# Joining the words of the float64 weights: two VectorE operations and one more ScalarE operation in place of three VectorE operations

## The chip, the cores and the metric

One core of a Trainium2 chip runs the whole program. The metric is the device time in microseconds (us), the median of several runs. TensorE (PE) does matrix products, VectorE (DVE) and ScalarE (ACT) elementwise work, GpSimd (POOL) some more of it, and SyncE (SP) issues the DMAs. Each engine works through its own instructions in a fixed order, and waits at its first instruction that is not ready.

## The reference

Three layers follow each other. All inputs and the output are float32, except that the MLP's three weights are drawn as float64.

```python
# 1. random-feature attention, 4 batches, 8 heads, 576 tokens, width 64
proj = x @ w_phi; proj -= max(abs(proj))
phi(x) = concat(exp(proj), exp(-proj))
kv = phi(k).T @ v; z = sum(phi(k)); attn = (phi(q) @ kv) / (phi(q) @ z + 1e-6)
# 2. gated MLP on 2304 tokens, 512 -> 1536 -> 512
xn = x / rms(x) * rms_g
x = (silu(xn @ w_gate) * (xn @ w_val)) @ w_out
# 3. soft mixture of experts: 8 experts, 4 slots each
logits = x @ phi; slots = softmax(logits, tokens).T @ x
out = softmax(logits, slots) @ (relu(slots @ w1[e]) @ w2[e])
```

## The kernel before

**First stage, keys.** The 2304 tokens are 18 tiles of 128. For each tile and each half of its heads, PE projects the keys (`P`, line 392), DVE takes the largest absolute value (`mx`, line 396) and subtracts it (`pr`, line 400), ACT computes both exponentials (`kp`, lines 413 and 414), and PE adds to `kv` and `z` (`kacc`, lines 437 and 446). Between these stand the steps of the first block of 384 queries: PE `P` (line 320), DVE `qmx` and `qpr` (lines 323 and 324), PE transposes, ACT exponentials (line 337), then per pair of heads the numerator `num` and the denominator `den`, a reciprocal on DVE (line 217), eight copies on ACT (line 222) and a product on DVE (`xraw`, line 223).

**Second stage, MLP.** Six blocks of 384 tokens go through 12 column tiles each: `pg` and `pv` (line 795), `t` (tanh on ACT, line 802, two products on DVE, lines 803 and 807), a split of `t` into a high part `hh` (ACT, line 101) and a remainder `hl` (POOL or DVE, line 104), and the sum over columns `acc` (lines 820 to 822). The queries of the next block are worked on between them. The mixture of experts follows.

**The weights.** They arrive as float64 words and are needed as float32 pairs. There are 18 pieces of 128x1024, here called g0, v0, o0, g1, ... o5 (gate, value and out weight of pair 0 to 5). Pieces g0 to o2 are converted in the first stage, g3 to o5 in the first MLP block. For each piece:

- a DMA loads `wraw`, 128x1024 pairs of 32-bit words (line 122); `raw[:, :, 1]` is the high word, `raw[:, :, 0]` the low word;
- ACT reads the high word as float32 and scales it by 2^-112 into `wt` (`scale`, line 126), which turns an 11-bit exponent into an 8-bit one;
- DVE shifts `wt` left by 3 (line 133), ors the sign in (line 135), and ors the low word's three top bits in (line 137), one operation per call of `join`;
- `parts` splits `wt` into a rounded part (ACT, line 101) and a remainder (POOL, line 104), after which `wt`'s buffer is free.

In the first stage there are three buffers for `wraw` and two for `wt`; in the MLP there are two for `wraw`, and one for `wt` in each of two pools that take turns. The calls of `conv_load`, `conv_scale`, `conv_join` and `conv_parts` are strewn over the loops by hand, and a scheduler then sets the order of instructions on each engine.

Of the kernel before, what the change touches and what calls it, by code (L numbers as in the profile page):

```python
# [10 lines left out]
AF = mybir.ActivationFunctionType  # L11
ALU = mybir.AluOpType
# [12 lines left out]
MF = DFF // 128  # L25
NJ = MF // 2
NPRE = 9
KCONV, MCONV = (3, 2), (2, 1)
NX = 3
NLEFT = 2  # L30
# [9 lines left out]
def batch_parts(i):  # L40

    t0, parts = i * 128, []
    r = 0
    while r < 128:
        b = (t0 + r) // SEQ
        end = min(128, (b + 1) * SEQ - t0)
        parts.append((b, r, end))
        r = end
    return parts
# [14 lines left out]
def tile_kernel(ctx: ExitStack, tc: tile.TileContext, q2T, qT, kT, v, wbd, wg, wv, wo, rmsg, phi, w1, w2, consts, out):  # L64
    nc = tc.nc
    PE, DVE, ACT, POOL, SP = nc.tensor, nc.vector, nc.scalar, nc.gpsimd, nc.sync

    def pool(stack, name, space=None, bufs=1, side="left"):
        kw = {} if space is None else {"space": space}
        if space is None:  # L70
            kw["side"] = side
        if space is not DRAM:
            kw["reuse_waits"] = "tile"
        return stack.enter_context(tc.tile_pool(name=name, bufs=bufs, **kw))
# [37 lines left out]
    class Conv:  # L112
# [11 lines left out]
        def scale(self):  # L124
            self.w = self.wp.tile([128, 1024], F32, tag="S", name="wt", bufs=self.bufs[1])
            ACT.activation(out=self.w, in_=self.raw[:, :, 1].bitcast(F32), func=AF.Copy, scale=2.0 ** -112)

        def join(self):

            n = self.n = self.n + 1  # L130
            w, hi, lo = self.w.bitcast(U32), self.raw[:, :, 1], self.raw[:, :, 0]
            if n == 1:
                DVE.tensor_scalar(out=w, in0=w, scalar1=3, scalar2=None, op0=ALU.logical_shift_left)
            elif n == 2:
                DVE.scalar_tensor_tensor(out=w, in0=hi, scalar=0x80000000, in1=w, op0=ALU.bitwise_and, op1=ALU.bitwise_or)  # L135
            else:
                DVE.scalar_tensor_tensor(out=w, in0=lo, scalar=29, in1=w, op0=ALU.logical_shift_right, op1=ALU.bitwise_or)  # L137

        def parts(self):
            j, nm = self.key  # L140
# [4 lines left out]
    loaded, convs, joined = [], [], []  # L145

    def conv_load(sp, bufs, *pools):

        key = next(conv_at, None)
        if key is not None:  # L150
            c = Conv(sp, pools[pieces.index(key) % len(pools)], key, bufs)
            c.load()
            loaded.append(c)

    def conv_scale():
        if loaded:
            convs.append(loaded.pop(0))
            convs[-1].scale()

    def conv_join():  # L160
        if convs:
            convs[-1].join()
            if convs[-1].n == 3:
                joined.append(convs.pop())

    def conv_parts():
        if joined:
            joined.pop(0).parts()
# [199 lines left out]
    with ExitStack() as pk:  # L368
# [148 lines left out]
        for i in range(TILES):  # L517
            k, kn = ks[i], ks[i + 1] if i + 1 < TILES else None
            if i + 3 < TILES:
                ks[i + 3].load()  # L520
            if i + 2 < TILES:
                ks[i + 2].load_v()
            if i % 2 and i // 2 + 2 < NPRE:
                conv_load(sp, KCONV, sp)
            parts = batch_parts(i)
            b = parts[0][0]
            ends = i * 128 + parts[0][2] == (b + 1) * SEQ

            def finish():
                ev = Evac(b)  # L530
                fillers.extend([lambda n=n: ev.turn(n) for n in range(3)])

            if len(parts) > 1:
                k.kv(parts[0])
                finish()
            if kn:
                kn.project()
                kn.largest(0)
                if i % 2 == 0:
                    conv_join()  # L540
                kn.less(0)
                kn.largest(1)
                conv_join()
                kn.less(1)
            k.kv(parts[-1])
            for hf in range(2):
                if kn:
                    kn.exps(hf)
                if hf == 0 and i % 2:
                    conv_parts()  # L550
                    conv_scale()
                if fillers:
                    fillers.pop(0)()
                for f in qsteps[2 * i + hf]:
                    f()
            if ends and len(parts) == 1:
                finish()
# [23 lines left out]
    class Own:  # L581
# [6 lines left out]
        def fill(self, f, h, k0, k1):  # L588
            w = NS * self.k
            n = NE - 1  # L590
            h = h.rearrange("p k (e s) -> p e k s", e=NE)
            own = self.t[:, 0:n * (w + SPE)].rearrange("p (e x) -> p e x", e=n)[:, :, 0:w].rearrange("p e (k s) -> p e k s", s=NS)
            f(own[:, :, k0:k1, 0:SPE], h[:, 0:n])
            own = self.t[:, n * w:].rearrange("p (k s) -> p k s", s=NS)
            f(own[:, k0:k1, NS - SPE:], h[:, n])
# [8 lines left out]
    with ExitStack() as p2:  # L604
# [194 lines left out]
        def gate(m, xs):  # L799
            g = wide("g", m, xs)  # L800
            t = mp.tile([128, BLK], F32, tag="t", name="t", bufs=2)
            ACT.activation(out=t, in_=g, func=AF.Tanh, scale=0.5)  # L802
            DVE.scalar_tensor_tensor(out=t, in0=t, scalar=1.0, in1=g, op0=ALU.add, op1=ALU.mult)  # L803
            return t
# [30 lines left out]
        for blk in range(NBLK):  # L835
            acc = [ps.tile([128, DM], F32, tag=f"acc{i}", name=f"acc{i}", bufs=1) for i in range(TPB)]
            qsteps, qnext = qnext or [], None
            if blk == 1:
                tctx.close()
                q1ctx.close()  # L840
                qp = pool(qctx, "qp", side="right")
                q = Reduced(qp, ps, 2, {"misc": 3})
                q.begin()
                qsteps = q.steps()
                sp = pool(pctx, "post", side="right")
                S_run = stp.tile([128, 2 * DM], F32, tag="S", name="S_run", bufs=1)[0:96, 0:DM]
            if blk == NBLK - 1:
                pctx.close()
                qctx.close()
                kl = pool(ctx, "kl", side="right")  # L850
                xw = pool(ctx, "xw", bufs=NX, side="right")
                upool[:0] = [xw] * NX
                sp = pool(pctx, "post", side="right")
            if blk:
                x2 = []
                for i in range(TPB):
                    y = sp.tile([128, DM], F32, tag="x2", name="x2", bufs=TPB)
                    ACT.activation(out=y, in_=acc_done[i], func=AF.Copy, scale=0.5)
                    x2.append(y)
                steps = post(blk - 1, x2)  # L860
            plan = [[] for _ in range(3 * MF + 1)]
            for n, f in qsteps:
                plan[n].append(f)
            for n, f in zip(PSLOTS, steps):
                plan[n].append(f)
            done = [0]

            def fill():
                done[0] += 1
                if blk == 0:  # L870
                    n = (done[0] - 1) % CEVERY
                    if n == 0:
                        conv_parts()
                        conv_scale()
                    conv_join()
                    if n == 2:
                        conv_load(sp, MCONV, sp, stp)
                for f in plan[done[0] - 1]:
                    f()

            for m in range(MF):
                if m + 1 == MF and blk + 1 < NBLK:
                    xs = split_block(xraw.pop(blk + 1))
                more = m + 1 < MF or blk + 1 < NBLK
                if more:
                    t = gate((m + 1) % MF, xs)
                fill()
                if more:
                    val((m + 1) % MF, xs, t)
                fill()  # L890
                if more:
                    for i in range(TPB):
                        out_tile(m, hs, acc, i)
                if more:
                    hs = split_h(t, blk == 0 and m < MF - 3)
                fill()
                if blk == NBLK - 1 and m % 2 == 1:
                    unit(min(len(units) + (NX + 2 if m == 1 else 2), 17 + NX))
                if m == MF - 3 and 3 <= blk + 2 < NBLK:
                    q = Reduced(qp, ps, blk + 2, {"misc": 3})  # L900
                    q.begin()
                    qnext = q.steps()
            acc_done = acc
# [157 lines left out]
```

## Time and profile before

| | |
|---|---|
| median of 3 runs | 755.49 us (755.3 to 758.66) |
| the profiled execution | 756.4 us, of which the span of its instructions is 754.5 us |
| PE busy | 720.1 us, 95% of the span |
| DVE, ACT, POOL busy | 444.4 us (59%), 353.4 us (47%), 121.2 us (16%) |
| TensorE's granted clock, mean | 0.987 |

An engine's busy share is an average over stages. Which engine sets the end is read from each stage: how long PE, which is the busiest, stands idle there, and what ended each of these waits.

### The profile page before, as it was taken

The numbers are of one execution on the slowest core, as the hardware profiler recorded it, in microseconds if no ns is written. First come the engines' busy times: TensorE is split into PE (matmuls) and PEld (weight loads), VectorE is DVE, ScalarE is ACT, GpSimd is POOL, SyncE is SP. The second block draws the span as 40 slices with busy tenths as digits, with TensorE's granted clock in tenths as the row PEclk, the third lists the DMA queues.
The fourth block names the chain that finished last, engine by engine and source line by source line (L and its number), as shares of the span: only waits on it lengthen the run. The fifth ranks groups of instructions, "written<-read, shape, count | busy, mean of one in ns | idle before, by whom it ended". The sixth has DMA issues, their size and how long they took to land.

```text
span 754.5 us, 12364 instructions
## 1 busy us (share of the span) xinstructions
PE 720.1 (95%) x4919; PEld 577.8 (77%) x4919; DVE 444.4 (59%) x816; ACT 353.4 (47%) x787; POOL 121.2 (16%) x70
## 2 busy tenths in 40 slices
PE   7998998997999999999999999999999999999994
PEld 4554555876788888898888988889888899988343
DVE  5897967699846556455565555645556453333313
ACT  5658765455644556434564346643465331212102
POOL 0222210245510211012110121101211010000000
PEclk9998999999999999999999999999999999999997
DMA  8664211544101100101000010000100046567798
GB/s 311 233 233 168 84 44 45 188 152 156 56 15 62 38 23 22 47 1 32 22 22 20 1 32 22 23 18 1 32 1 2 9 168 242 204 235 282 280 374 315
DMA packets 25145, 79.45 MB, mean 105 GB/s; under 512 B 2688, under 2 KB 13376, under 8 KB 18688
## 3 DMA queue, kind: packets, MB, share of 16 engines
q1 hardware_dynamic: 24864, 77.79, 29.5%
q10 hardware_dynamic: 224, 0.88, 0.4%
q8 instruction: 38, 0.62, 0.3%
q14 instruction: 19, 0.16, 0.1%
HBM read 71.99 MB, written 6.67 MB: 104 GB/s over the span
## 4 chain that ended last, share of the span: by engine, by line
PE 75%; DVE 11%; DMA 5%; ACT 5%; issue 2%; POOL 0%; SPq 0%; ACTq 0%; DVEq 0%
PE pv L795 18%; PE pg L795 17%; PE acc L820 6%; PE acc L821 6%; PE acc L822 6%; PE num L204 4%; PE kacc L437 3%; DMA eu<-in_w_dram 2%; DVE wt L135 2%; PE P L392 2%; PE den L212 2%; DVE wt L137 2%; PE kacc L446 2%; DMA wraw<-in_wg_dram 2%; ACT e L222 1%
## 5 line engine op out<-in xcount | busy, mean ns | idle before, releaser
L795 PE MATMUL pv<-xnh,wv 128*128 128x384 f32 x576 | 151.5, 344 | 1.1 <-DVE t L807 1.1
L795 PE MATMUL pg<-xnh,wg 128*128 128x384 f32 x576 | 150.1, 342 | 0.2 <-ACT xnh L101 0.2
L795 PEld LDWEIGHTS pv<-xnh,wv 128*128 128x128 f32 x576 | 103.1, 188 | 8.6 <-issue 6.7
L795 PEld LDWEIGHTS pg<-xnh,wg 128*128 128x128 f32 x576 | 104.7, 188 | 5.9 <-ACT xnh L101 0.6
L795 PE MATMUL pv<-xnl,wv 128*128 128x384 f32 x288 | 97.7, 339 | 0.0
L795 PE MATMUL pg<-xnl,wg 128*128 128x384 f32 x288 | 97.5, 338 | 0.0
L278 POOL PARTITION_ALL_REDUCE qe<-qe x32 | 50.0, 1562 | 247.3 <-ACT qe L277 227.7
L820 PE MATMUL acc<-wo,hh 128*128 128x512 f32 x216 | 88.4, 409 | 1.0 <-ACT hh L101 0.9
L822 PE MATMUL acc<-wo,hl 128*128 128x512 f32 x216 | 85.5, 396 | 1.9 <-POOL hl L104 1.9
L821 PE MATMUL acc<-wo,hh 128*128 128x512 f32 x216 | 85.8, 397 | 0.0
L101 ACT CAST hh<-t 128x384 fp32r<-128x384 f32 x72 | 36.7, 510 | 85.6 <-PE acc L821 68.7
L803 DVE SCALAR_TENSOR_TENSOR t<-t,pg 128x384 f32<-128x384 f32 x72 | 39.7, 551 | 52.6 <-ACT t L802 52.5
L802 ACT ACTIVATE t<-pg 128x384 f32<-128x384 f32 x72 | 35.1, 487 | 63.2 <-PE pg L795 63.2
L104 DVE TENSOR_TENSOR hl<-t,hh 128x384 fp32r<-128x384 f32 x62 | 34.5, 557 | 48.0 <-ACT hh L101 45.5
L222 ACT COPY qe<-qe 32x192 f32<-32x192 f32 x128 | 44.8, 350 | 31.7 <-DVE qe L217 30.4
L807 DVE TENSOR_TENSOR t<-t,pv 128x384 f32<-128x384 f32 x72 | 39.7, 552 | 30.2 <-PE pv L795 28.9
L795 PEld LDWEIGHTS pg<-xnl,wg 128*128 128x128 f32 x288 | 54.0, 188 | 0.3 <-DVE xnl L104 0.3
L795 PEld LDWEIGHTS pv<-xnl,wv 128*128 128x128 f32 x288 | 54.0, 188 | 0.1
L822 PEld LDWEIGHTS acc<-wo,hl 128*128 128x128 f32 x216 | 40.6, 188 | 12.5 <-POOL hl L104 2.7
L437 PE MATMUL kacc<-kp,vt 128*64 128x256 f32 (+1 forms) x320 | 44.1, 400 | 4.0 <-ACT kp L414 4.0
L820 PEld LDWEIGHTS acc<-wo,hh 128*128 128x128 f32 x216 | 40.7, 189 | 9.2 <-ACT hh L101 2.0
L821 PEld LDWEIGHTS acc<-wo,hh 128*128 128x128 f32 x216 | 40.7, 188 | 6.4
(188 smaller groups left out, 1091.0 us busy)
## 6 DMA issues: line engine op xcount, KB each, us to landing
eu<-in_w_dram SPq DMA_DIRECT2D x32, 1024.0 KB, 6.2
wraw<-in_wg_dram SPq DMA_DIRECT2D x6, 1024.0 KB, 6.0
wraw<-in_wv_dram SPq DMA_DIRECT2D x6, 1024.0 KB, 6.3
wraw<-in_wo_dram SPq DMA_DIRECT2D x6, 1024.0 KB, 4.9
qraw<-in_qT_dram SPq DMA_DIRECT2D x32, 192.0 KB, 2.3
raw<-in_kT_dram SPq DMA_DIRECT2D x18, 256.0 KB, 4.0
vt<-in_v_dram SPq DMA_DIRECT2D x18, 256.0 KB, 3.2
out_dram<-ob SPq DMA_DIRECT2D x18, 256.0 KB, 3.4
```

Of the source, the lines that this page charges most:

```text
L101: ACT.copy(out=hi, in_=src)
L104: (lo_eng or POOL).tensor_tensor(out=lo, in0=src, in1=hi.bitcast(F32), op=ALU.subtract)
L222: ACT.copy(out=rd[64 * hh + 32 * r:64 * hh + 32 * r + 32, g], in_=dn[o:o + 32])
L278: POOL.partition_all_reduce(e[:, 0], e[:, 1], channels=128, reduce_op=bass_isa.ReduceOp.absmax)
L437: PE.matmul(out=kva[o0:o0 + 64, hh // 2], lhsT=self.vt[r0:r1, h], rhs=kp[r0:r1, hh].rearrange("p s f -> p (s f)"), start=first and hh < 2, ...
L795: PE.matmul(out=p, lhsT=w[:, a, c], rhs=x, start=n == 0, stop=n == 11)
L802: ACT.activation(out=t, in_=g, func=AF.Tanh, scale=0.5)
L803: DVE.scalar_tensor_tensor(out=t, in0=t, scalar=1.0, in1=g, op0=ALU.add, op1=ALU.mult)
L807: DVE.tensor_tensor(out=t, in0=t, in1=wide("v", m, xs), op=ALU.mult)
L820: PE.matmul(out=acc[i], lhsT=hh[:, s], rhs=w[:, 0], start=m == 0, stop=False)
L821: PE.matmul(out=acc[i], lhsT=hh[:, s], rhs=w[:, 1], start=False, stop=False)
L822: PE.matmul(out=acc[i], lhsT=hl[:, s], rhs=w[:, 0], start=False, stop=m == MF - 1)
```

## The change

The low word is no longer shifted by DVE. A second ACT operation, right after `scale`, reads it as an unsigned integer, multiplies it by 0.93 times 2^-29, and writes it back in place, rounded to an integer from 0 to 7. DVE then does the left shift by 3 and the or with these bits in one operation (first join), and ors the sign in (second join). So a piece has two joins and not three. In the first stage the join at even tiles is gone, in the MLP the one that stood beside `scale`.

```diff
+LOW = 0.93 * 2.0 ** -29
...
         def scale(self):
             self.w = self.wp.tile([128, 1024], F32, tag="S", name="wt", bufs=self.bufs[1])
             ACT.activation(out=self.w, in_=self.raw[:, :, 1].bitcast(F32), func=AF.Copy, scale=2.0 ** -112)
+            lo = self.raw[:, :, 0]
+            ACT.activation(out=lo, in_=lo, func=AF.Copy, scale=LOW)
...
             if n == 1:
-                DVE.tensor_scalar(out=w, in0=w, scalar1=3, scalar2=None, op0=ALU.logical_shift_left)
-            elif n == 2:
+                DVE.scalar_tensor_tensor(out=w, in0=w, scalar=3, in1=lo, op0=ALU.logical_shift_left, op1=ALU.bitwise_or)
+            else:
                 DVE.scalar_tensor_tensor(out=w, in0=hi, scalar=0x80000000, in1=w, op0=ALU.bitwise_and, op1=ALU.bitwise_or)
-            else:
-                DVE.scalar_tensor_tensor(out=w, in0=lo, scalar=29, in1=w, op0=ALU.logical_shift_right, op1=ALU.bitwise_or)
...
-            if convs[-1].n == 3:
+            if convs[-1].n == 2:
                 joined.append(convs.pop())
...
                 kn.project()
-                kn.largest(0)
-                if i % 2 == 0:
-                    conv_join()
-                kn.less(0)
+                kn.shift(0)
                 kn.largest(1)
                 conv_join()
                 kn.less(1)
...
                         conv_parts()
                         conv_scale()
-                    conv_join()
+                    else:
+                        conv_join()
```

The scheduler places the instructions anew. Up to line 126 a line of the kernel stands one higher in the numbers of the change (127 is the old `scale`, 129 the new operation on the low word), behind `scale` it differs by up to four; 137 and 139 are the two joins. Three places matter below.

ScalarE, in the first stage, where the first block's first copies (`e` from `e`, x8) stand. Before:

```order
L214 COPY xraw<-num 128x384
L414 ACTIVATE kp<-pr 128x4x128
L337 ACTIVATE e_531<-T 128x2x128 x2
L101 CAST wv_842<-wt 128x1024
L126 ACTIVATE wt<-wraw 128x1024
L222 COPY e_298<-e_298 32x192 x8
```

Now:

```order
L216 COPY xraw<-num 128x384
L102 CAST wv_842<-wt 128x1024
L339 ACTIVATE e_532<-T 128x2x128 x2
L129 ACTIVATE wraw<-wraw 128x1024
L102 CAST wo_1006<-wt 128x1024
L224 COPY e_298<-e_298 32x192 x8
```

The `scale` of g2, which stood right ahead of the eight copies, is behind them now; the low word of g2 and the rounding of o1 stand ahead of them.

ScalarE, some six instructions of `kp` later, ahead of the tile whose `kp` comes next. Before:

```order
L461 COPY kvs_792<-kacc_426 128x512
L126 ACTIVATE wt<-wraw 128x1024
L413 ACTIVATE kp<-pr 128x4x128
L414 ACTIVATE kp<-pr 128x4x128
L485 COPY kv_794<-kvt 128x2x2x64
```

Now:

```order
L463 COPY kvs_792<-kacc_426 128x512
L127 ACTIVATE wt<-wraw 128x1024
L129 ACTIVATE wraw<-wraw 128x1024 x2
L415 ACTIVATE kp<-pr 128x4x128
L416 ACTIVATE kp<-pr 128x4x128
L487 COPY kv_794<-kvt 128x2x2x64
```

The low words of v2 and of o2 both stand ahead of `kp` now.

VectorE, from the joins of v1 to the first block's second reciprocal. Before:

```order
L323 TENSOR_REDUCE qmx<-P 128x2
L133 TENSOR_SCALAR wt<-wt 128x1024
L324 TENSOR_TENSOR qpr<-P,qmx 128x256
L135 SCALAR_TENSOR_TENSOR wt<-wraw,wt 128x1024
L396 TENSOR_REDUCE mx<-P 128x4 x2
L400 TENSOR_TENSOR pr<-P,mx 128x512 x2
L137 SCALAR_TENSOR_TENSOR wt<-wraw,wt 128x1024
L133 TENSOR_SCALAR wt<-wt 128x1024
L216 TENSOR_SCALAR e_298<-den 128x192
L135 SCALAR_TENSOR_TENSOR wt<-wraw,wt 128x1024
L217 RECIPROCAL e_298<-e_298 128x192
```

Now:

```order
L325 TENSOR_REDUCE qmx<-P 128x2
L137 SCALAR_TENSOR_TENSOR wt<-wt,wraw 128x1024
L326 TENSOR_TENSOR qpr<-P,qmx 128x256
L398 TENSOR_REDUCE mx<-P 128x4 x2
L402 TENSOR_TENSOR pr<-P,mx 128x512 x2
L139 SCALAR_TENSOR_TENSOR wt<-wraw,wt 128x1024
L137 SCALAR_TENSOR_TENSOR wt<-wt,wraw 128x1024
L218 TENSOR_SCALAR e_298<-den 128x192
L139 SCALAR_TENSOR_TENSOR wt<-wraw,wt 128x1024
L219 RECIPROCAL e_298<-e_298 128x192
```

One join fewer stands ahead of the two `mx`, and one fewer behind the two `pr`. PE's order of the MLP is the same in both, and so is its work.

## Rows read from the trace of the kernel before

**Rows 1.** Busy time by stretch: first stage, first MLP block, and behind it
```profile
core 0: us, PE busy (x) PEld busy (x) DVE busy (x) ACT busy (x) POOL busy (x), PEclk, DMA share, GB/s
20.00:135.00 115.00, 107.41 (x1000) 62.26 (x1000) 93.37 (x152) 77.89 (x160) 21.27 (x9) 0.97 0.39 128
135.00:210.00 75.00, 68.12 (x408) 57.24 (x407) 65.42 (x78) 41.29 (x83) 34.92 (x17) 1.00 0.40 139
...
240.00:400.00 160.00, 159.71 (x974) 138.64 (x973) 92.55 (x178) 81.67 (x195) 27.27 (x17) 1.00 0.09 26
```

**Rows 2.** PE's waits from 0 to 240 us: total, times, longest
```profile
PE P L320 <- DVE qpr L324: 3.0, 1, 3.0
PE num L204 <- ACT e L337: 2.7, 1, 2.7
PE acc L822 <- POOL hl L104: 1.9, 2, 1.1
PE P L320 <- DVE kv L483: 1.3, 2, 0.7
PE pv L795 <- DVE t L807: 1.1, 1, 1.1
```

**Rows 3.** Groups of instructions from 0 to 210 us: busy us, mean ns, idle before
```profile
L135 DVE SCALAR_TENSOR_TENSOR wt<-wraw,wt 128x1024 uint32<-128x1024 uint32 x18 | 27.6, 1534 | 0.2
...
L133 DVE TENSOR_SCALAR wt<-wt 128x1024 uint32<-128x1024 uint32 x18 | 22.6, 1258 | 6.9 <-ACT wt L126 6.9
...
L126 ACT ACTIVATE wt<-wraw 128x1024 f32<-128x1024 f32 x18 | 20.9, 1161 | 14.7 <-DMA wraw<-in_wg_dram 6.9 <-POOL wv L104 3.4 <-DMA wraw<-in_wv_dram 2.6
```

**Rows 4.** DVE in order of time: start us, us, instruction, idle before and releaser
```profile
38.21 2.70 DVE L133 TENSOR_SCALAR wt<-wt 128x1024 uint32<-128x1024 uint32 x1
...
49.80 3.42 DVE L135 SCALAR_TENSOR_TENSOR wt<-wraw,wt 128x1024 uint32<-128x1024 uint32 x1
...
65.53 0.56 DVE L223 TENSOR_TENSOR xraw<-xraw,e 128x384 f32<-128x384 f32 x1 [1.73 <-ACT e L222]
```

**Rows 5.** POOL in order of time
```profile
37.99 2.37 POOL L104 TENSOR_TENSOR wo<-wt,wo 128x1024 fp32r<-128x1024 f32 x1 [2.71 <-ACT wo L101]
49.77 2.37 POOL L104 TENSOR_TENSOR wg<-wt,wg 128x1024 fp32r<-128x1024 f32 x1 [9.41 <-ACT wg L101]
```

**Rows 6.** PE in order of time, runs of one instruction merged
```profile
14.06 1.95 PE L437 MATMUL kacc<-kp,vt 128*64 128x256 f32 x16
...
43.03 0.70 PE L320 MATMUL P<-wbd_f,qraw 128*128 128x256 f32 x2 [0.70 <-DVE kv L483]
...
44.31 1.95 PE L437 MATMUL kacc<-kp,vt 128*64 128x256 f32 x16
...
62.82 0.71 PE L392 MATMUL P<-wbd_f,raw 64*128 64x128 f32 x6
66.58 1.19 PE L320 MATMUL P<-wbd_f,qraw 128*128 128x256 f32 x2 [3.05 <-DVE qpr L324]
...
69.27 3.68 PE L437 MATMUL kacc<-kp,vt 128*64 128x256 f32 x16
...
76.65 1.95 PE L437 MATMUL kacc<-kp,vt 128*64 128x256 f32 x16
```

**Rows 7.** Busy time by stretch, columns as in rows 1
```profile
68.00:70.00 2.00, 2.00 (x14) 1.58 (x14) 1.86 (x5) 1.99 (x5) 0.49 (x1) 0.50 0.00 0
40.00:100.00 60.00, 55.10 (x513) 33.43 (x514) 54.15 (x85) 45.64 (x96) 12.19 (x6) 0.94 0.44 143
```

**Rows 8.** ACT in order of time
```profile
14.15 0.61 ACT L414 ACTIVATE kp<-pr 128x512 f32<-128x512 f32 x1
...
61.58 1.17 ACT L126 ACTIVATE wt<-wraw 128x1024 f32<-128x1024 f32 x1 [2.48 <-POOL wv L104]
62.65 2.86 ACT L222 COPY e<-e 32x192 f32<-32x192 f32 x8
...
181.29 1.15 ACT L126 ACTIVATE wt<-wraw 128x1024 f32<-128x1024 f32 x1 [2.55 <-DMA wraw<-in_wg_dram]
```

## The prediction

> **What bounds the kernel now.** I read the busy time by stretch first, to find where PE stands idle. From 20 to 135 us, the first stage, PE is busy for 107.41 of 115 us; from 135 to 210 us, where the first MLP block runs and the last nine pieces are converted, for 68.12 of 75; from 240 to 400 us for 159.71 of 160 [rows 1]. So behind the conversions the kernel is PE's own work, and the change, which leaves PE's work alone, can win only what PE waits for ahead of 210 us: 7.6 us and 6.9 us. Whatever PE gains there moves all that follows forward by the same amount.
>
> Next, the list of PE's waits. Its long entries are `P` of the queries waiting for `qpr` (3.0 us, once) and for the copies `kv` (1.3 us, twice), `num` waiting for ACT (2.7), `acc` for POOL's `hl` (1.9) and `pv` for DVE's `t` (1.1) [rows 2]. No matrix product waits for a weight: the conversion harms PE only by standing in DVE's and ACT's queues ahead of something else.
>
> Then, what a conversion costs these queues. DVE's first join, the shift, takes 1258 ns in the mean and the second 1534, ACT's `scale` 1161 [rows 3]. The means hide something: the shift at 38.21 us took 2.70 us because it began 0.2 us after POOL's remainder of o0 (37.99, 2.37 us), and the join at 49.80 us took 3.42 us, beside POOL's remainder of g1 (49.77) [rows 4, 5]. Each ended some 0.6 or 1.1 us behind POOL's operation, which is its own length. So a join that meets a remainder stands still until POOL is through, with all of DVE's queue behind it.
>
> Last, the longest wait followed back in order of time. PE stops after 63.5 us and goes on at 66.58 us [rows 6]. `qpr` stood in DVE's queue behind `xraw`, which started at 65.53 us after waiting for ACT's eight copies; these ran from 62.65 us, behind the `scale` of g2, which waited 2.48 us for POOL to free a `wt` buffer [rows 4, 8]. And the wait is paid twice: in the stretch from 68 to 70 us the granted clock is 0.50 [rows 7], 1.2 in place of 2.4 GHz, and the 16 `kacc` at 69.27 us take 3.68 us where those at 76.65 us take 1.95 [rows 6].
>
> **The change, part by part.**
>
> *DVE.* 18 shifts go: 22.6 us of busy time [rows 3], of which 18 x 0.6 us is their own work and the rest waiting for POOL. The new first join has two tensors in, like the old second and third, so I price it as one: 1.1 us alone, up to 3.4 where it meets POOL [rows 4], and 1.5 in the mean, no change.
>
> *ACT.* 18 operations on the low word come. None with integers in and out stands in the trace. The nearest row is `scale`, same tile, same stride, 1161 ns [rows 3]; started back to back it holds the queue for 1.07 us (61.58 to 62.65, [rows 8]). I take 1.1 us; the range keeps 1.0 to 2.37 us, the upper end being what the same tile takes on POOL [rows 5]. The ScalarE page of the Trainium skill ("ScalarE: Activation LUTs", What ACT_TABLE_LOAD costs) gives 186 ns and 0.833 ns per element, by which the operation would be an estimated 1.04 us and the sum below would move by less than half a microsecond; no row shows its rate for integers.
>
> *First stage, gains.* (a) At 43.03 us PE waited 0.70 us for `kv` [rows 6], which stood in DVE's queue behind the shift that met POOL [rows 4, 5]. In the new order no join stands there while POOL runs. The other wait for `kv` is alike; both make 1.3 us [rows 2]. (b) The `scale` of g2 is behind the eight copies now (first place shown), and the join of 3.42 us stands ahead of POOL's operation. The wait of 3.05 us goes, and with it the slow clock: `kacc` 1.73 us, and half of the 2.69 us of `P` between 66.58 and 69.27, 1.35; both about 3.1. Sum 6.1.
>
> *First stage, costs.* (c) The low word of g0 stands ahead of the `kp` at 14.15 us. That `kp` ends at 15.8 instead of 14.8; PE, which starts `kacc` at 14.06, wants it half way through, at 15.1 [rows 6, 8]: 0.7 us. (d) `P` of the queries now follows `den` directly. PE is there at 62.82 us [rows 6] less the 0.7 of (a), 62.1. The `qpr` that it needs is still behind `xraw` and its copies. Without the wait of 2.48 us and with DVE some 1.5 us ahead of then I put the copies' end at 61.1 instead of 65.5, and `qpr` 1.2 us behind, at 62.3: 0.2 us stay. (e) The second half's `pr` then stands behind the second `xraw`, whose copies take another 2.86 us [rows 8]; I put PE's arrival at `P` 1.4 us ahead of it, bounds 0 and 2.9. (f) `scale` of v2 and two low words, 3.3 us in one row, stand ahead of `kp` (second place shown) where there was one operation. From 40 to 100 us ACT is busy for 45.64 of 60 us [rows 7], and six new operations leave it 7.8 us of air; I put 2.4 of the 3.3 us on the path, bounds 0 and 3.3. Sum of costs 4.7.
>
> First stage: 1.3 + 6.1 - 4.7 = 2.7 us won.
>
> *First MLP block.* `pv` waited for a `t` that stood behind a join blocked by POOL: 1.1 us won. `num` waited 2.7 us because ACT stood at the `scale` of g5 until its DMA landed (2.55 us, at 181.29 [rows 8]); that `scale` is now behind the exponentials, and I leave 1.1 us of it: 1.6 won. Of `acc`'s 1.9 us for `hl` [rows 2] I take 0.5, since fewer ACT and DVE operations are late ahead of it. Against this, the `scale` of v5 now stands ahead of an `hh` and waits for its own DMA: between 0 and the 2.55 us of its sister, 1.4. Won: 1.8 us.
>
> *Moved DMAs.* A `wraw` buffer comes free one join earlier and two loads on SP change places with a neighbour. PE waits for no weight [rows 2], so nothing is counted; were this cover gone, it would be up to 2.55 us at ACT again.
>
> **Sum.** 756.4 - 2.7 - 1.8 = 751.9 us for an execution like the profiled one. The median of the runs is 0.9 us below it, so the forecast is **751.0 us**, 0.6% faster.
>
> **The rivals.**
>
> *ScalarE gives it back (same).* ACT is in the path of every tile by `kp`, and all nine new operations of the first stage come on top: 9 x 1.07 = 9.6 us against gains of 7.4; in the MLP 1.4 against 3.2. Then 756.4 - 10.6 + 11.0 = 756.8, median **755.9**. For it: ACT is busy for 76% from 40 to 100 us [rows 7]. Against it: ACT's waits there, 14 us, are where the scheduler put most of them. The ScalarE page of the Trainium skill (Rules for kernel authors) sends multiplications to VectorE, as faster per element; that speaks for this rival. In this kernel the removed operation took 1258 ns in the mean on VectorE and its neighbour on ScalarE 1161 [rows 3], so the trace does not bear the rule out here.
>
> *Slow integers (slower).* If an integer operation takes 2.37 us, six of them are 14.2 us, all of the 14.4 us that ACT has free from 40 to 100 us [rows 7]. `kp` is late by 1.3 us six times, 7.8 us, and one of the waits is long enough for the clock to fall, 3.1 us as seen: 751.9 + 10.9 = 762.8, median **761.9**. It decides from about 1.9 us on, where six times 0.75 us eat the 4.5 us won. Nothing in the trace shows it.
>
> *All waits go (faster still).* No new wait forms: 756.4 - 7.4 - (1.1 + 2.7 + 1.9) = 743.3, median **742.4**. Against it: the second `xraw` and the three ACT operations in one row are in the order.
>
> That the change computes something else would not alter the time; the operations are there whatever the bits are.
>
> **How the numbers follow.** Half a per cent, 3.8 us, is about what a measurement of this kernel can tell from no change: below 751.7 is faster, above 759.3 slower. The forecast gets 0.52 (0.40 of it below 751.7 and 0.12 above, since its own terms (d) to (f) are good for 3 us either way), the ScalarE rival 0.27 (0.22 same, 0.02 faster, 0.03 slower), slow integers 0.09, all waits gone 0.12. Faster 0.54, same 0.34, slower 0.12. The range goes from 743.5, a little above the last case's value, to 758.0, with the ScalarE rival's spread and without the slow integers; the forecast's own range is 747 to 754.
>
> **What would show it.** The low-word operation at 1.0 to 1.2 us, 18 times; the shift gone and both joins with a mean of 1.5 us or less; no wait of 3 us for `qpr` near 65 us, and the granted clock at 1.00 from 60 to 80 us; `kv` and `qpr` gone from the head of PE's waits, and new waits of `kacc` for `kp` near 15 and 75 us in their place. It is wrong if that low-word row reads 2 us, if the clock still falls in the first stage, or if the gain comes from behind 240 us.

## The result, and the profile after

The changed kernel took **751.14 us** in the median of 10 runs (750.72 to 753.04), against 757.95 us (755.3 to 762.63, 10 runs) for the kernel before. The ratio is 0.9912, 95% interval 0.9889 to 0.9936: 0.9% faster. The forecast was 751.0 us.

The profiled execution took 753.04 us, the longest of the ten, with a span of 750.4 us. Busy time by stretch, columns as in [rows 1]; the stretch from 40 to 100 us answers to [rows 7]:

```profile
20.00:135.00 115.00, 107.62 (x1017) 61.94 (x1015) 87.95 (x147) 85.39 (x168) 22.22 (x9) 0.99 0.39 128
135.00:210.00 75.00, 70.65 (x422) 61.68 (x421) 55.46 (x71) 53.73 (x98) 33.70 (x17) 0.98 0.39 139
240.00:400.00 160.00, 159.71 (x971) 138.43 (x971) 91.65 (x176) 82.13 (x196) 27.50 (x17) 1.00 0.10 27
40.00:100.00 60.00, 54.91 (x541) 31.89 (x540) 51.92 (x83) 53.90 (x107) 16.53 (x7) 1.00 0.48 157
```

DVE lost 5.4 us of busy time in the first stage and 10.0 us in the MLP block, ACT gained 7.5 and 12.4. From 240 to 400 us PE is as busy as before. (Of the 4.1 us between the two spans 1.5 lie behind 700 us, where the granted clock fell in the profiled execution of before and not in this one; in the repeated profile below it falls there too.) The groups that answer to [rows 3]:

```profile
L137 DVE SCALAR_TENSOR_TENSOR wt<-wt,wraw 128x1024 uint32<-128x1024 uint32 x18 | 27.7, 1540 | 11.1 <-ACT wraw L129 9.4 <-issue 1.6
L139 DVE SCALAR_TENSOR_TENSOR wt<-wraw,wt 128x1024 uint32<-128x1024 uint32 x18 | 27.5, 1528 | 0.1
L127 ACT ACTIVATE wt<-wraw 128x1024 f32<-128x1024 f32 x18 | 21.0, 1164 | 11.1 <-DMA wraw<-in_wg_dram 3.4 <-DMA wraw<-in_wv_dram 3.0 <-POOL wg L105 2.9
L129 ACT ACTIVATE wraw<-wraw 128x1024 uint32<-128x1024 uint32 x18 | 20.8, 1160 | 0.4 <-DMA wraw<-in_wo_dram 0.4
```

The low-word operation takes 1160 ns, as `scale` does with 1164; the new first join takes 1540, as the old second did with 1534. PE's waits from 0 to 240 us, to be held against [rows 2]:

```profile
PE kacc L439 <- ACT kp L416: 5.2, 6, 1.8
...
PE pg L794 <- DVE t L802: 1.9, 1, 1.9
PE T L337 <- DVE qpr L326: 1.5, 1, 1.5
PE P L322 <- DVE kv L485: 1.3, 2, 0.8
PE P L394 <- DVE pr L402: 1.0, 2, 0.5
PE P L322 <- DVE qpr L326: 0.9, 1, 0.9
...
PE acc L821 <- POOL hl L105: 0.4, 1, 0.4
PE num L206 <- ACT e L339: 0.3, 1, 0.3
```

The 3.0 us for `qpr` are 0.9 now, `num` waits 0.3 in place of 2.7, `acc` 0.4 in place of 1.9, and `pv` not at all. New are 1.5 and 1.9 us for `qpr` and `t`, both near 192 us. The longest entry, `kp`, was the longest entry of the program's own work in the kernel before too, where [rows 2] and the prediction leave it out:

```profile
PE kacc L437 <- ACT kp L414: 4.0, 4, 1.8
```

Its two long waits, 1.42 us at the start and 1.80 us near 130 us, stand in both profiles. Two short ones (0.52 and 0.30 us) are gone and four have come (0.23, 0.82, 0.77 and 0.19 us): 1.2 us more in all. PE in order of time, where [rows 6] had the long stop:

```profile
65.61 0.67 PE L322 MATMUL P<-wbd_f,qraw 128*128 128x256 f32 x2 [0.88 <-DVE qpr L326]
66.21 1.16 PE L394 MATMUL P<-wbd_f,raw 64*128 64x128 f32 x16
67.30 1.95 PE L439 MATMUL kacc<-kp,vt 128*64 128x256 f32 x16
...
72.22 1.13 PE L394 MATMUL P<-wbd_f,raw 64*128 64x128 f32 x14 [0.54 <-DVE pr L402]
...
79.84 1.08 PE L439 MATMUL kacc<-kp,vt 128*64 128x256 f32 x8 [0.82 <-ACT kp L416]
81.69 0.65 PE L439 MATMUL kacc<-kp,vt 128*64 128x256 f32 x4 [0.77 <-ACT kp L416]
```

The 16 `kacc` behind the stop take 1.95 us in place of 3.68: the granted clock stays at 1.00 from 40 to 100 us (0.94 before).

**Where the time went.** Two marks that PE passes in every kernel of this study cut the run: the first `P`, whose start hangs on the first DMA, and the two `r` (line 345 before), one at the end of the first stage, one at the end of the MLP block's queries. This table is the measure for all the experiments; each length is one `r` start less the mark before it, in the profiled execution.

| kernel | first `P` to first `r` | first to second `r` |
|---|---|---|
| before | 119.93 | 111.42 |
| after | 119.24 | 108.83 |
| after, repeated | 117.64 | 109.00 |
| `first_only` | 118.88 | 111.53 |
| `mlp_only` | 124.65 | 108.03 |
| `act_extra` | 121.38 | 111.30 |
| `two_joins` | 118.25 | 112.29 |
| `w3_before` | 123.29 | 111.86 |
| `before_rem` | 120.52 | 103.74 |
| `rem_dve` | 119.12 | 102.59 |
| `rem_dve_all` | 118.26 | 102.20 |
| `rem_mix` | 122.36 | 102.68 |
| `w3_rem` | 117.83 | 102.13 |
| `rem_g0` | 121.41 | 102.51 |

The second column is steady: kernels with the same conversion in the MLP lie within 1 us. The first is not: the same instructions differ by up to 4.7 us (before and `mlp_only`). Of these, 1.6 us come from the start, which is slow in six of the fourteen profiles (last section), and the rest from the granted clock, which falls to 0.50 between 108 and 114 us in `mlp_only` and not in before. So only whole runs, a wait followed in order of time, or profiles with the same start can be compared there. With the fast start, before and `before_rem` need 119.93 and 120.52 us and the repeat of the change 117.64: 2.3 to 2.9 us less.

### The profile page after: what moved, and what is told of

Its sections match the earlier page's. It is cut to its first block, busy times and chain, and to the rows that moved or that the text cites. A ratio compares the mean times of both kernels' runs of the same rounds, so it can differ in the third digit from the quotient of the medians.

```text
span 750.4 us, 12367 instructions
## 1 busy us (share of the span) xinstructions
PE 718.8 (96%) x4919; PEld 578.4 (77%) x4919; DVE 425.6 (57%) x798; ACT 371.7 (50%) x805; POOL 120.9 (16%) x70
## 4 chain that ended last, share of the span: by engine, by line
PE 74%; ACT 10%; DVE 6%; DMA 6%; issue 1%; POOL 1%; SPq 0%; DVEq 0%; ACTq 0%; POOLq 0%
PE pv L794 18%; PE pg L794 17%; PE acc L819 6%; PE acc L820 6%; PE acc L821 6%; PE num L206 4%; PE kacc L439 3%; DMA eu<-in_w_dram 2%; PE den L214 2%; ACT e L224 2%; PE kacc L448 2%; DVE wt L137 2%; DVE wt L139 1%; PE P L394 1%; DMA wraw<-in_wv_dram 1%
```

## The experiments

Two theories stood at the start. Theory 1: what is won comes from the order in the queues, above all from the `scale` of g2 that no longer waits for POOL ahead of the eight copies. Theory 2: it comes from VectorE's saved time as such.

**The two stages apart.** One flag per piece chooses the old or the new joins (`key[0] < 3` or `>= 3`):

```diff
+            self.two = key[0] < 3
...
+            if self.two:
+                lo = self.raw[:, :, 0]
+                ACT.activation(out=lo, in_=lo, func=AF.Copy, scale=LOW)
```

> The new joins for the nine pieces of the first stage alone, the three old joins for the nine of the MLP. Theory 1 (both stages win, as forecast): PE's first-stage milestones are as after the change (P of the queries waits under 1 us near 65 us, kacc at about 73 us in place of 76.65), the MLP block is as before; 2 to 3.5 us won, ratio 0.995 to 0.998. Rival (the first stage gives all it wins back by 134 us, as the one profile of the changed kernel reads): ratio 0.999 to 1.002.

> The three old joins in the first stage, the new ones for the nine pieces of the first MLP block alone. Theory 1 (both stages win): the first stage is as before with its wait of about 3 us for qpr, the MLP block wins what it wins after the change, 2.6 us (pv and acc no longer wait, num waits 0.3 in place of 2.7 us); ratio 0.995 to 0.998. Rival (all of the gain is the MLP block's): ratio 0.989 to 0.993, as with the whole change.

`first_only` took 754.68 us (ratio 0.9971, 0.9955 to 0.9988), `mlp_only` 754.75 (0.997, 0.9948 to 0.9993). So each stage wins about 0.3%, some 2.2 us, and both rivals of the expectations fall. The two sum to 0.6% where the whole change gives 0.9%; the intervals allow the same.

**Each half of the change alone.** `act_extra` keeps ScalarE's new operation and gives VectorE its third one back; `two_joins` has VectorE's saving and not ScalarE's operation (it leaves the three low bits out). The scheduler orders every kernel anew, so each edit also moves instructions that it does not name; what stood ahead of what is therefore read from each trace.

```diff
-                DVE.scalar_tensor_tensor(out=w, in0=lo, scalar=29, in1=w, op0=ALU.logical_shift_right, op1=ALU.bitwise_or)
+                DVE.scalar_tensor_tensor(out=w, in0=lo, scalar=0, in1=w, op0=ALU.logical_shift_right, op1=ALU.bitwise_or)
```

> The third VectorE join stays (it ors the low word in without shifting it), and ScalarE's operation on the low word comes on top: ScalarE does what it does after the change, VectorE what it did before. In this order the scale of g2 is behind the first block's eight copies, as after the change. Theory 1 (the queue order: the first-stage gain is that this scale no longer waits for POOL ahead of the copies): no wait of about 3 us of P for qpr near 65 us, granted clock 1.00 from 60 to 80 us, kacc at about 76 us started 1 to 3 us sooner than before; in the MLP block pv and acc wait as before, and r of the last tokens ends no sooner; ratio to before 0.995 to 1.003. Theory 2 (VectorE's saved time as such): the wait for qpr stays or comes back in another place, nothing is won anywhere and 18 x 1.1 us of ScalarE are paid in part; ratio 1.000 to 1.008.

> The third join is dropped and nothing takes its place: the three low bits of each weight are left out. VectorE does one shift and one sign join per piece, ScalarE nothing new. Here the scale of g2 still stands ahead of the eight copies. Theory 1 (the queue order): P still waits 1 to 3 us for qpr near 65 us and at least a third of the first-stage gain is missing, the MLP block wins 2 to 4 us; ratio 0.993 to 0.998. Theory 2 (VectorE's saved time as such, less what ScalarE pays): this is the change without its cost, so faster than it in both stages, by what kacc waits for kp there (about 2 to 3 us); ratio 0.984 to 0.989.

`act_extra`: 757.73 us, ratio 1.0011 (0.9988 to 1.0034). `two_joins`: 755.39 us, 0.9981 (0.9959 to 1.0003). Neither half does what both do. That `two_joins`, which has no ScalarE operation to pay, lies behind the whole change rules theory 2 out in its simple form. Theory 1 missed there too: it gave the MLP block 2 to 4 us, and by the table the block lost 0.9, with waits of 4.4 us of `num` for ACT. `act_extra`'s ratio lies in the ranges of both theories. PE of `two_joins`, in order of time:

```profile
67.91 0.67 PE L320 MATMUL P<-wbd_f,qraw 128*128 128x256 f32 x2 [2.13 <-DVE qpr L324]
```

and that of `act_extra`:

```profile
67.17 0.70 PE L323 MATMUL P<-wbd_f,qraw 128*128 128x256 f32 x2 [0.93 <-ACT xraw L217]
...
75.52 3.54 PE L440 MATMUL kacc<-kp,vt 128*64 128x256 f32 x16 [1.17 <-DVE kvs L462]
```

In `two_joins` a `scale` still stands ahead of the copies (61.44 us), and a join now stands between `qmx` and `qpr` (66.22 us): the stop stays, with a third fewer joins on VectorE. In `act_extra` the `scale` is gone from there, but the third join stands between `qmx` and `qpr` (64.97 us). The wait is short because PE comes late and not because `qpr` comes soon: this `P` starts 62.55 us behind the first one, where it was 62.39 before and is 59.09 in the repeat of the change. Another stop comes at 75 us, and the clock falls there (16 `kacc` in 3.54 us).

**The `scale` alone out of the way.** The kernel before with a third `wt` buffer:

```diff
-KCONV, MCONV = (3, 2), (2, 1)
+KCONV, MCONV = (3, 3), (2, 1)
```

> The kernel before with three buffers for wt in the first stage in place of two, and no other edit: three joins, ScalarE without the low words. The scale of g2 need not wait for POOL and is now issued well ahead of the eight copies. Theory 1 (that scale's wait was the 3 us stop): the wait of 3.05 us of P for qpr near 65 us falls under 1 us, the granted clock stays at 1.00 there, and the first stage wins 2 to 4 us without one VectorE operation less; ratio 0.995 to 0.998. Rival (qpr is late because VectorE is behind with its joins, whatever ScalarE does): a wait of over 2 us for qpr or pr stays; ratio 0.999 to 1.003.

758.38 us, ratio 0.9995 (0.9961 to 1.0028): no gain that the runs can tell. PE still stops for 2.16 us where it stopped for 3.05, and the `kacc` behind still takes 3.68 us. Theory 1 in the form "that `scale` was the stop" has failed. DVE shows why:

```profile
64.22 0.56 DVE L223 TENSOR_TENSOR xraw<-xraw,e 128x384 f32<-128x384 f32 x1 [0.61 <-ACT e L222]
64.70 0.42 DVE L323 TENSOR_REDUCE qmx<-P 128x2 f32<-128x256 f32 x1
65.03 1.22 DVE L137 SCALAR_TENSOR_TENSOR wt<-wraw,wt 128x1024 uint32<-128x1024 uint32 x1
66.16 0.41 DVE L324 TENSOR_TENSOR qpr<-P,qmx 128x256 f32<-128x256 f32 x1
```

The wait of `xraw` for the copies is 0.61 us and not the 1.73 of [rows 4]. But the third join, which stood ahead of `xraw` before, in time in which DVE had to wait for the copies anyway, now stands between `qmx` and `qpr`. From 65.03 to 66.16 us it holds `qpr` up for 1.1 us; without it PE's wait would be an estimated 1.0 us. (Starts are not compared with those of before here: this profile has the slow start.) So the stop had two causes, one behind the other: an ACT that waited, worth some 0.9 us, and on DVE a join too many, worth some 1.1. The change takes away both: its `qpr` runs at 65.04 us, right behind `qmx`, and PE waits 0.88 us. That both had to go fits these three kernels and the change, but it is read from their traces; no kernel here took away both in another way.

**The change again.**

> The changed kernel, nothing edited, beside the others on one chip. If the result is the kernel's and not of one chip or one day: ratio 0.988 to 0.994. In its profile the waits of PE are those of the first profile within 0.3 us each; where the granted clock is 0.50 may differ (near 120 us and 195 us if it is set by the order of the work, elsewhere if it is chance).

751.66 us, ratio 0.9914 (0.9885 to 0.9943). The waits are those of the first profile, and the granted clock falls again near 118 and 192 us.

**POOL out of the MLP block.** The new 1.5 and 1.9 us near 192 us come from one join. POOL, then DVE, of the change:

```profile
187.53 2.39 POOL L105 TENSOR_TENSOR wg<-wt,wg 128x1024 fp32r<-128x1024 f32 x1 [0.47 <-ACT wg L102]
```

```profile
187.64 3.36 DVE L137 SCALAR_TENSOR_TENSOR wt<-wt,wraw 128x1024 uint32<-128x1024 uint32 x1
190.93 0.41 DVE L326 TENSOR_TENSOR qpr<-P,qmx 128x256 f32<-128x256 f32 x1
```

The join began 0.11 us behind POOL's remainder and ended 1.08 us behind it. `rem_dve` gives the nine remainders of the MLP to VectorE, `rem_dve_all` all 18:

```diff
-            split(u[:, 0], u[:, 1], self.w, hi_eng=ACT, lo_eng=POOL)
+            split(u[:, 0], u[:, 1], self.w, hi_eng=ACT, lo_eng=POOL if j < 3 else DVE)
```

> The changed kernel with the remainders of the nine MLP pieces on VectorE in place of POOL, so no join of the MLP block can meet a long POOL operation. Theory 1 (a join that meets a remainder stands still until POOL is through, and that is what is left of the waits in the MLP block): the joins of the MLP block all take 1.0 to 1.2 us, the waits of T for qpr (1.5 us) and pg for t (1.9 us) near 192 us go and with them the granted clock of 0.5 behind them; 2 to 4 us faster than the changed kernel, ratio 0.984 to 0.990. Rival (VectorE's queue is late from its own work): nine more operations of 1.1 us make new waits of the same size; ratio 0.990 to 0.996.

> The changed kernel with all 18 remainders on VectorE. In the first stage VectorE is busier (57 of 60 us from 40 to 100 us it would be, had no join waited for POOL; the joins should now read 1.1 us in place of up to 3.3). Theory 1 (what blocks the joins is POOL): VectorE's busy time falls or stays although it has 18 operations more, and the first stage is no slower; ratio 0.982 to 0.990. Rival (VectorE is the bound of the first stage by its own work): the first stage loses 2 to 6 us; ratio 0.990 to 0.998.

`rem_dve`: **745.53 us**, ratio 0.9836 (0.9798 to 0.9873), some 6 us better than the change. The MLP block, where PE had been busy for 70.65 of 75 us:

```profile
135.00:210.00 75.00, 74.48 (x454) 66.30 (x454) 61.16 (x88) 54.36 (x100) 13.35 (x9) 1.00 0.39 139
```

and, from 135 to 212 us, the joins and the first of the three groups of remainders:

```profile
L139 DVE SCALAR_TENSOR_TENSOR wt<-wraw,wt 128x1024 uint32<-128x1024 uint32 x9 | 12.6, 1403 | 0.1
L137 DVE SCALAR_TENSOR_TENSOR wt<-wt,wraw 128x1024 uint32<-128x1024 uint32 x9 | 11.4, 1269 | 3.7 <-ACT wraw L129 3.7
...
L105 DVE TENSOR_TENSOR wo<-wt,wo 128x1024 fp32r<-128x1024 f32 x3 | 3.7, 1221 | 0.3 <-ACT wo L102 0.3
```

The remainder takes 1.22 us on VectorE, 2.4 to 2.7 on POOL. The waits for `qpr` and `t` are gone, and so is the slow clock behind them. The joins are not all at 1.2 us, as was expected: some meet POOL's short `hl`. `rem_dve_all` (746.13 us, 0.9841, 0.9803 to 0.9879) is no better than `rem_dve`. Its first stage shows a join without POOL (both groups 0 to 135 us):

```profile
L137 DVE SCALAR_TENSOR_TENSOR wt<-wt,wraw 128x1024 uint32<-128x1024 uint32 x9 | 11.0, 1221 | 0.5 <-ACT wt L127 0.5
L139 DVE SCALAR_TENSOR_TENSOR wt<-wraw,wt 128x1024 uint32<-128x1024 uint32 x9 | 11.0, 1220 | 0.0
```

But DVE is busier there (94.17 us from 20 to 135, the change 87.95), and a new wait of 1.82 us for DVE comes at 115 us.

**Does that need the change?**

> The kernel before, with its three joins, and the remainders of the nine MLP pieces on VectorE in place of POOL. Theory 1 (what blocks a join is POOL, in either form of the join): the MLP block wins here as well, its joins read 1.2 us and its shift 0.7, pv and acc wait less; VectorE is busy for some 70 of 75 us, so less is won than the 6 us by which this edit made the changed kernel faster; ratio 0.993 to 0.998. Rival (the edit pays only with the two joins, since three joins and a remainder fill VectorE): ratio 0.999 to 1.005.

750.22 us, ratio 0.9894 (0.987 to 0.9919): one edit of the kernel before, with three joins, is worth at least as much as the change, and more than theory 1 had put. Its MLP block takes 103.74 us against 111.42; with the two joins 102.59 against 108.83. So once POOL is out of the way, the change is worth 1.2 us there and not 2.6: about half of what it won in this block was that fewer joins met POOL, as far as lengths that scatter by up to 1 us can tell. (A remainder that ends sooner also frees its `wt` sooner, but in the MLP block of the kernel before no ACT instruction waits for POOL.) In the first stage, which keeps its remainders on POOL, the stop of 3.0 us for `qpr` is still in `before_rem`, and the change still pays.

**Three tries to go further.**

> The changed kernel with all remainders on VectorE except the three of pair 2, which stay on POOL. With all 18 on VectorE PE stood 1.1 us sooner at 87 us and lost it by 122 us, where the remainders of v2 and o2 stand in VectorE's queue. Theory 1: this keeps the one and not the other, 1 to 2 us faster than with the MLP's nine alone; ratio 0.980 to 0.984. Rival (the first stage is bound by VectorE's own work): ratio 0.984 to 0.988, no better.

> The changed kernel with the remainders of the MLP pieces on VectorE and three buffers for wt in the first stage. In the kernel before a third buffer won nothing. Theory 1 (there a join between qmx and qpr still held the queue; here no join stands there): the wait of P for qpr near 65 us, 0.9 us, goes, and ScalarE's waits for POOL too; 0 to 1.5 us faster than without the third buffer; ratio 0.980 to 0.984. Rival (ScalarE's low words ahead of kp are what is left): no gain, ratio 0.983 to 0.987.

> The changed kernel with the remainders of the MLP pieces on VectorE, and the piece g0 alone converted in the old way (three VectorE operations, no low word on ScalarE). Theory 1 (the low word of g0 ahead of kp costs PE 0.7 us at the start, as forecast): kacc in the second tile is not split, P near 18 us starts 0.5 to 0.7 us sooner against the first P, and 0.3 to 0.7 us are left at the end; ratio 0.982 to 0.985. Rival: the 0.7 us are lost again behind, at the next wait; ratio 0.983 to 0.987.

`rem_mix`: 750.91 us (0.9896, 0.9869 to 0.9923), worse: the new order makes `P` wait 1.65 us for `kv` and `kacc` 2.33 us for `kp`, each with a slow clock behind it. Both theories missed. `w3_rem`: 746.01 us (0.9834, 0.9809 to 0.9859), as `rem_dve`; the wait for `qpr` falls to 0.31 us, but nothing is left of it at the end that the runs can tell. `rem_g0`: 746.38 us (0.9847, 0.9813 to 0.988), no gain either. The ratios of these two lie in the ranges of both theories and decide nothing. Its start does show the cost of the low word of g0, PE by time:

```profile
13.44 1.16 PE L399 MATMUL P<-wbd_f,raw 64*128 64x128 f32 x16
14.53 1.95 PE L444 MATMUL kacc<-kp,vt 128*64 128x256 f32 x16
...
18.47 1.16 PE L399 MATMUL P<-wbd_f,raw 64*128 64x128 f32 x8
```

`P` comes 13.80 us behind the first one (4.67), in `rem_mix`, with that low word, 14.50 (18.94 less 4.44): 0.70 us. It is lost again from 66 us on, where the new order brings back a wait of 2.2 us for `qpr`, as the rival said.

The best kernel is `rem_dve`, with `rem_dve_all` and `w3_rem` beside it.

## Why the prediction held, and where it did not

**The bound, the prices: right.** Against the first `P`, 3.3 and 4.7 us of the gain lie ahead of the second `r` in the two profiles of the change. Behind it lie 1.5 and 1.1 us, less than the scatter of that part, which takes 516.6 to 520.5 us in the fourteen profiles. The low-word operation was put at 1.1 us; it holds ACT's queue for 1.06 (13.87 to 14.93 us) and is busy 1.16. So "slow integers" falls. The estimate by the Trainium skill's ScalarE page ("ScalarE: Activation LUTs", What ACT_TABLE_LOAD costs), 1.04 us, is 0.12 below the busy time here; the trace agrees roughly, for integers too.

**First stage, forecast 2.7 us.** `first_only` measures 2.2 us (757.12 x 0.0029; 0.9 to 3.4 by the interval). Step by step, in the repeated profile, against the first `P`:

- (a) failed. Forecast: the wait of 0.70 us for `kv` goes, "no join stands there while POOL runs". None does, but in the first profile the first join of g1 stands there, cannot begin before its low word is through on ACT (43.89 us), and the copy `kv` starts at 45.04 behind it. PE waits 0.81 us, and the two waits for `kv` still make 1.3. (In the kernel before, too, a join that met nothing, 1.21 us at 41.43 us, stood between the blocked shift and `kv`; the step left it out.) Moving an operand to another engine made a wait of its own; the step looked only at POOL.
- (b), (d) and (e): the steps around the long stop gave 6.1 less 0.2 less 1.4, 4.5 us. PE is 0.50 us ahead at the `kacc` that was at 44.31 us [rows 6] (now 44.13, with the first `P` at 4.51 and not 4.19), and 5.69 us at that of 76.65 (now 71.28): 5.2 won. (b) was about right in size, though it named one cause of two. (d) was 0.88 us, not 0.2: the copies, put to end at 61.1 us or 56.9 behind the first `P`, ended at 62.07, 57.6 behind it, since the low word of g2 and the rounding of o1 stand ahead of them on ACT. (e) was 0.55, not 1.4.
- (c) 0.7, measured 0.69 against before and 0.70 by `rem_g0`, but not as the wait that was forecast. PE waits for no `kp` there; the scheduler has split the 16 `kacc` in its order, and the split costs the time. The repeated profile, then the end of this piece before, which started at 14.06 us [rows 6] (3.57 us against 2.88):

```profile
14.38 1.08 PE L439 MATMUL kacc<-kp,vt 128*64 128x256 f32 x8
15.39 0.62 PE L448 MATMUL kacc<-kp,small 128*32 128x256 f32 x2
15.94 1.08 PE L439 MATMUL kacc<-kp,vt 128*64 128x256 f32 x8
16.95 1.06 PE L448 MATMUL kacc<-kp,small 128*32 128x256 f32 x14
17.95 1.13 PE L322 MATMUL P<-wbd_f,qraw 128*128 128x256 f32 x4
```

```profile
16.94 1.13 PE L320 MATMUL P<-wbd_f,qraw 128*128 128x256 f32 x4
```

- Not forecast: between there and the `kacc` at 44 us PE needs 26.18 us where it needed 27.37, for the same 216 instructions, with no wait in either but those for `kv`. The new order goes through 30 runs of like instructions, the old through 36. These 1.2 us, which no step names, pay for (c) and more; no kernel here changes PE's order alone.
- (f) 2.4, measured 0.82 and 0.77, that is 1.6: three ACT operations in one row from 75.41 to 78.61 us, then `kp`. Over all of `kp`'s waits the loss is 1.2.
- Not forecast: near 118 us the granted clock falls to 0.50 in both profiles of the change, and 16 `kacc` take 3.27 and 3.54 us where they took 1.95. That takes back 1.3 to 1.6 us in them. `before_rem`, with the old first stage, shows the same, so it is not shown to be a cost of the change.

**MLP block, forecast 1.8 us**, measured 2.6 and 2.4 in the two profiles, 2.3 by `mlp_only`. `pv` won its 1.1. `num` won 2.4 (forecast 1.6) and `acc` with its `hl` 1.5 (forecast 0.5). The loss of 1.4 us at the `scale` of v5 did not come: it waited for no DMA. In its place the join of v5 met POOL and cost 1.5 and 1.9 us of waits and a slow clock. That a join that meets a remainder stands still was the prediction's own reading [rows 4, 5]; it was used for the first stage and not asked of the new order in the MLP. The page "SBUF — State Buffer" of the Trainium skill (Who interferes with whom) says that a VectorE operation with two SBUF inputs contends with a GpSimd one that reads SBUF, and calls the ports that they share an exclusive lock; the 3.36 us at 187.64, POOL's rest and 1.08, agree.

**The sum.** The step that failed in size is the last, "the median of the runs is 0.9 us below": the median of before is 757.95 us here, 1.5 above the profiled execution, and later comparisons give 757.1 to 757.4. The median of three runs was low. So the forecast of 751.0 came of a gain of 4.5 us from 755.5; what was measured is 6.8 us from 757.95 (4.8 to 8.4 by the interval). Two errors cancelled, and that forecast and result agree to 0.1 us is luck.

Of the 2.3 us by which the gain was too small, 0.7 are the MLP block. In the mean, three profiles that run the old first stage unchanged (before, `mlp_only`, `before_rem`) need 121.7 us for it, four with the new one (after, its repeat, `first_only`, `rem_dve`) 118.7. But one of the three and three of the four have the slow start. With the same fast start the new first stage is 2.3 to 2.9 us shorter, about as forecast, though out of other parts. The remaining 1.6 us are not located. The profiled execution of before was a good one, and the runs of the change lie within 2.3 us, those of before within 7.3: the change may also remove some of the bad executions. Why a given execution is bad is open.

**The rivals.** "ScalarE gives it back" describes `act_extra` (1.0011), in which ScalarE pays and VectorE saves nothing; the change as a whole is faster, clear of the noise. "All waits go" fell, since (d) to (f) stand in the trace.

## What to carry to other kernels

A wait in a list names the last of several things that were late: before a gain is booked for removing it, ask what stands right behind it in the same queue, as the join did behind the copies. Where VectorE and GpSimd work side by side, look first at the long GpSimd operations that VectorE's operations run into; taking nine of them off GpSimd was worth as much as thinning VectorE's work by a third of its joins, and cost one line. An operand that moves to another engine brings that engine's queue into the wait.

## What was not expected of the hardware

- At the start, the first eight `kacc`, at about 10 us, take 1.08 us in eight profiles and 1.97 or 1.98 in six, whatever the kernel (after 1.98, its repeat 1.08), while the granted clock in the windows reads 1.00. That alone moves an execution by 1.3 to 1.8 us.
- The granted clock does not fall only behind long stops. Near 118 us PE had last waited for 0.49 us. In `w3_rem` the same instructions follow the same wait, and the clock stays. The repeated change, then `w3_rem`:

```profile
117.03 3.54 PE L439 MATMUL kacc<-kp,vt 128*64 128x256 f32 x16
```

```profile
116.11 0.46 PE L394 MATMUL P<-wbd_f,raw 64*128 64x128 f32 x2 [0.49 <-DVE pr L402]
...
118.19 1.95 PE L439 MATMUL kacc<-kp,vt 128*64 128x256 f32 x16
```

  All four profiles with the change's own first stage (after, its repeat, `first_only`, `rem_dve`) show it there, so it is not plain chance; but so does `before_rem`, and not before, whose first stage is the same. What sets it is open.
- ScalarE's operation on integers, in place and with a stride of 8 bytes, takes as long as the float one beside it: 1160 and 1164 ns.
